# Two-layer gated MLP behind linear attention: the gated product's tiles placed 64 bytes higher in SBUF, with a smaller DMA scratch

## The chip, the cores and the metric

The kernel runs on one core of one Trainium2 chip. The metric is the device time of one execution in microseconds; before the change three runs took 992.68, 993.05 and 998.37 us, with a median of 993.05 us.

## What is computed

Attention with an exponential feature map gives 2304 tokens of 512 values (4 sequences of 576 tokens, 8 heads of 64). Two gated layers follow, each with three weight matrices of 512 x 1536, 512 x 1536 and 1536 x 512. All is in float32.

```python
def _moe_ref(x, w_gate, w_val, w_out):        # layer 1
    g = x @ w_gate
    silu = g * (1.0 / (1.0 + np.exp(-g)))
    val = x @ w_val
    return (silu * val @ w_out).astype(np.float32)

def _moe2_ref(x, w_gate, w_val, w_out):       # layer 2
    gate = 1.0 / (1.0 + np.exp(-(x @ w_gate)))
    val = x @ w_val
    return (gate * val @ w_out).astype(np.float32)

x = attention(q, k, v, w_phi)                 # 2304 x 512
return _moe2_ref(_moe_ref(x))
```

## The kernel before, in words

The attention takes the first 150 us or so and the two gated layers the rest. Each layer is done in two passes over the tokens, one for each half of its 1536 hidden values, so there are four passes, `hh` = 0 to 3; `hh` 0 and 1 are layer 1, `hh` 2 and 3 are layer 2. A pass goes through five blocks of tokens, four of 512 and one of 256, and in each block through three groups `p` of 256 hidden values. A block and a group make a **unit**, so a pass has twelve full units and three half units, and the two layers have the same units in the same number.

A unit has two kinds of matrix multiplication on TensorE. Every float32 factor is held as a high and a low tile of type float32r (names ending in `h` and `l`), and every product is made of three matmuls: high by high, high by low, low by high.

- **Products** (line 1024, `product`): x by `w_gate` and x by `w_val`, in a form with seven block products instead of eight. A full unit has 84 of them, a half unit 48. The stationary operand is a 128 x 128 piece of the tiles `w0h`, `w0l`, `w1h`, ... `w2l`; the moving one is 256 columns of `xh` or `xl`. They write PSUM banks `a` and `b`.
- **Output matmuls** (lines 1099 and 1101, `accumulate`): the gated product of the unit before, held in the tiles `uh0`, `ul0`, `uh1`, `ul1`, by the output weights `o0h` ... `o2l`, into the PSUM banks `c` and `d`. A full unit has 24, in trains of 12, 9 and 3 that stand between groups of 48, 12 and 24 products. In layer 1 (line 1099) the output weights are stationary and 512 columns of `u` move (256 in the small block). In layer 2 (line 1101) 128 columns of `u` are stationary and 512 columns of the output weights move:

```python
if hh < 2:
    nc.tensor.matmul(ps[:, :n], a[:, k], x, start=st, stop=sp)   # line 1099: o stationary, u moves
else:
    nc.tensor.matmul(ps, x[:, k], a, start=st, stop=sp)          # line 1101: u stationary, o moves
```

Between the two, ScalarE copies, gates and rounds (lines 1044, 1062, 579) and VectorE adds, multiplies and takes the low parts (lines 1050, 1067, 573). The tiles that they share with TensorE are `c0` and `c1` (products and their sums) and the four `u` tiles. All six come from the pool `u`, which is opened at line 468, behind the pools of the weights (`w0`, `w1`), of the staging pieces and of the first set of x tiles (`x0`). The pool of the second set of x tiles (`x1`) is opened on top of it when the attention's tiles are gone; `w2` is on the other side of SBUF.

The order of all instructions is written out in a table of times (`TIMES`), and each engine works through its own in that order. Every DMA is issued by SyncE's queue.

A matmul that begins while the next one's stationary piece is being loaded reads SBUF at the same time as that load: the moving columns of one matmul and the stationary columns of the one behind it. "Place" below is a tile's byte address in a partition modulo 256, as the built programs have it. All slices that the matmuls take begin at multiples of 512 bytes into their tile, so that a tile's place is the place of every operand in it.

Of the kernel before, what the change touches and what calls it, by code (L numbers as in the profile page):

```python
# [10 lines left out]
F32 = mybir.dt.float32  # L11
# [9 lines left out]
P = 128  # L21
# [432 lines left out]
def body(ctx: ExitStack, tc: tile.TileContext, qT, kT, v, w_phi2, wpk, out):  # L454
    nc = tc.nc
# [9 lines left out]
    pools = {w: ctx.enter_context(tc.tile_pool(name=w, bufs=1)) for w in ("w0", "w1")}  # L465
    stage = ctx.enter_context(tc.tile_pool(name="stage", bufs=1))
    pools["x0"] = ctx.enter_context(tc.tile_pool(name="x0", bufs=1))
    pools["u"] = ctx.enter_context(tc.tile_pool(name="u", bufs=1))

    xT = [dram.tile([KC, P, S], F32, name=f"xT{b}") for b in range(B)]  # L470
    den = [dram.tile([H, S], F32, name=f"den{b}") for b in range(B)]
# [836 lines left out]
```

## Time and profile before

| | |
|---|---|
| median of three runs | 993.05 us |
| the profiled execution | 996.62 us, of which 994.5 us are its span |
| TensorE (PE) busy | 980.9 us, 99% of the span |
| TensorE weight loads (PEld) | 891.5 us, 90% |
| VectorE (DVE) / ScalarE (ACT) | 692.4 us, 70% / 527.2 us, 53% |
| granted TensorE clock | 1.00 of full speed, the 2.4 GHz level |

Matmuls are pipelined: one begins some 110 to 240 ns after the one before it, and lasts longer than that. So the rate of TensorE is read from the starts in the timeline, and not from the duration of one. The time between two starts is called an interval here. Two starts of the timeline that stand n matmuls apart, divided by n, give the mean interval over them; the timeline has starts to 0.01 us.

### The profile page before, as it was taken

How to read it: one execution, taken by the hardware profiler on the slowest of the kernel's cores; microseconds unless marked ns; L12 is line 12 of the kernel's file. 1: busy time of each engine (PE TensorE's matmuls, PEld its weight loads, DVE VectorE, ACT ScalarE, POOL GpSimd, SP SyncE). 2: the span in 40 equal slices, each digit the busy share in tenths (PEclk: the TensorE clock that was granted, in tenths of full speed). 3: DMA queues.
4: the chain of work that ended last, by engine and by line, in shares of the span. 5: the costliest groups of instructions: out<-in, count | busy, mean ns of one | idle time of the engine just before them, and what ended most of it. 6: DMA issues, size and time to landing. Idle time of an engine off the chain costs nothing.

```text
span 994.5 us, 20911 instructions
## 1 busy us (share of the span) xinstructions
PE 980.9 (99%) x8632; PEld 891.5 (90%) x8632; DVE 692.4 (70%) x1220; ACT 527.2 (53%) x977; POOL 38.8 (4%) x40
## 2 busy tenths in 40 slices
PE   7999999999999999999999999999999999999998
PEld 6777778999999999999999999999999999999997
DVE  6999888938757795368787897486677834555343
ACT  5988977535545564264454574455546534334321
POOL 1433210000000000000000000000000000000000
PEclk9999999999999999999999999999999999999999
DMA  7566876436535532066554442446416002132011
GB/s 239 167 216 211 262 240 197 149 126 182 196 118 153 183 96 83 1 198 213 155 174 134 167 156 77 141 141 197 144 70 191 23 21 86 64 128 86 1 44 42
DMA packets 67551, 136.00 MB, mean 137 GB/s; under 512 B 9408, under 2 KB 35712, under 8 KB 67456
## 3 DMA queue, kind: packets, MB, share of 16 engines
q1 hardware_dynamic: 67456, 134.68, 42.4%
q8 instruction: 67, 1.10, 0.4%
q14 instruction: 28, 0.23, 0.1%
HBM read 94.66 MB, written 39.99 MB: 135 GB/s over the span
## 4 chain that ended last, share of the span: by engine, by line
PE 95%; DVE 3%; DMA 1%; ACT 0%; issue 0%; SPq 0%; DVEq 0%; ACTq 0%
PE a L1024 30%; PE b L1024 23%; PE c L1101 8%; PE c L1099 8%; PE d L1099 8%; PE d L1101 6%; PE d L787 5%; PE c L724 3%; PE w L688 3%; DVE sub L697 1%; DVE m L695 1%; PE w L751 1%; DMA xT<-nd 1%; DMA x<-kT 0%; ACT eq L771 0%
## 5 line engine op out<-in xcount | busy, mean ns | idle before, releaser
L1050 DVE TENSOR_TENSOR c<-b,c 128x512 f32<-128x512 f32 x96 | 66.0, 687 | 118.9 <-PE b L1024 109.9
L1062 ACT ACTIVATE c<-c 128x256 f32<-128x256 f32 x96 | 50.3, 525 | 147.0 <-DVE c L1050 147.0
L1044 ACT COPY c<-a 128x512 f32<-128x512 f32 x96 | 56.4, 587 | 111.9 <-PE a L1024 109.3
L573 DVE TENSOR_TENSOR ul<-c,uh 128x512 fp32r<-128x512 f32 (+1 forms) x120 | 75.8, 635 | 33.3 <-ACT uh L579 32.5
L579 ACT CAST uh<-c 128x512 fp32r<-128x512 f32 (+1 forms) x120 | 69.3, 580 | 41.6 <-DVE c L1067 33.3
L1024 PE MATMUL a<-xh,w0h 128*128 128x256 f32 x288 | 80.7, 280 | 0.0
L1024 PE MATMUL a<-xh,w1h 128*128 128x256 f32 x288 | 80.5, 280 | 0.0
L1024 PE MATMUL a<-xh,w2h 128*128 128x256 f32 x288 | 80.5, 279 | 0.0
L1024 PE MATMUL a<-xl,w0h 128*128 128x256 f32 x288 | 80.3, 279 | 0.0
L1024 PE MATMUL a<-xl,w2h 128*128 128x256 f32 x288 | 80.3, 279 | 0.0
L1024 PE MATMUL a<-xl,w1h 128*128 128x256 f32 x288 | 80.3, 279 | 0.0
L1024 PE MATMUL a<-xh,w0l 128*128 128x256 f32 x288 | 80.2, 279 | 0.0
L1024 PE MATMUL a<-xh,w2l 128*128 128x256 f32 x288 | 80.2, 279 | 0.0
L1024 PE MATMUL a<-xh,w1l 128*128 128x256 f32 x288 | 80.2, 278 | 0.0
L1067 DVE TENSOR_TENSOR c<-c 128x256 f32<-128x256 f32 (+1 forms) x96 | 52.9, 555 | 29.4 <-ACT c L1062 29.4
L1024 PE MATMUL b<-xh,w0h 128*128 128x256 f32 x224 | 62.5, 279 | 0.0
L1024 PE MATMUL b<-xh,w0l 128*128 128x256 f32 x224 | 62.4, 279 | 0.0
L1024 PE MATMUL b<-xh,w2l 128*128 128x256 f32 x224 | 62.4, 279 | 0.0
L1024 PE MATMUL b<-xh,w1l 128*128 128x256 f32 x224 | 62.4, 279 | 0.0
L1024 PE MATMUL b<-xl,w0h 128*128 128x256 f32 x224 | 62.4, 279 | 0.0
L1024 PE MATMUL b<-xh,w1h 128*128 128x256 f32 x224 | 62.4, 278 | 0.0
L1024 PE MATMUL b<-xl,w1h 128*128 128x256 f32 x224 | 62.4, 278 | 0.0
(183 smaller groups left out, 3028.5 us busy)
## 6 DMA issues: line engine op xcount, KB each, us to landing
raw<-wpk SPq DMA_DIRECT2D x72, 512.0 KB, 5.0
wf<-wcv SPq DMA_DIRECT2D x40, 256.0 KB, 2.8
a<-wf SPq DMA_DIRECT2D x20, 512.0 KB, 5.3
b<-xo SPq DMA_DIRECT2D x16, 512.0 KB, 6.1
part<-o SPq DMA_DIRECT2D x13, 512.0 KB, 6.2
o<-part SPq DMA_DIRECT2D x13, 512.0 KB, 4.7
wfo<-wcv SPq DMA_DIRECT2D x20, 256.0 KB, 4.9
v<-v SPq DMA_DIRECT2D x18, 264.0 KB, 7.3
```

What stands on the lines that cost most here:

```text
L573: nc.vector.tensor_tensor(out=lo, in0=src, in1=hi, op=ALU.subtract)
L579: nc.scalar.copy(hi, src)
L688: nc.tensor.matmul(r["ps"][:, i, n, c], r["x"][d, c, n * P:(n + 1) * P], w2[d], start=True, stop=True)
L724: nc.tensor.matmul(kv[qd, b][h // 2][u * 64:(u + 1) * 64, c * P:c * P + VW], e[r0:r1, h % 2, n, h // 2, s, u], r["v"][r0:r1, n, h], start= ...
L787: nc.tensor.matmul(pn[i * w:(i + 1) * w, :m], f, e[:, h, c, :m], start=(c == 0), stop=(c == 1))
L1024: nc.tensor.matmul(o, f[:, c], x[:, c], start=k == first and w == 0 and c == 0 and m == 0, stop=c == 1 and m == 2, skip_group_check=True)
L1044: nc.scalar.copy(part_of(r, d), parts(r, src))
L1050: nc.vector.tensor_tensor(out=c, in0=parts(r, "zy x"[d]), in1=c, op=ALU.add)
L1062: nc.scalar.activation(o, g, AF.Silu if hh < 2 else AF.Sigmoid)
L1067: nc.vector.tensor_tensor(out=o, in0=v, in1=places(r, j, 0, d)[1], op=ALU.mult)
L1099: nc.tensor.matmul(ps[:, :n], a[:, k], x, start=st, stop=sp)
L1101: nc.tensor.matmul(ps, x[:, k], a, start=st, stop=sp)
```

## The change

Three lines open room in SBUF, and one makes the DMA scratch smaller:

```diff
     pools["u"] = ctx.enter_context(tc.tile_pool(name="u", bufs=1))
+    pools["u"].tile([P, 16], F32, name="gap")
+    rest = ctx.enter_context(tc.tile_pool(name="rest", bufs=1))
+    rest.tile([P, 112], F32, name="rest")
...
-    nc = bacc.Bacc("TRN2", target_bir_lowering=False, num_devices=1)
+    nc = bacc.Bacc("TRN2", target_bir_lowering=False, num_devices=1, dynamic_dma_scratch_size=1024)
```

`gap` is 64 bytes in a partition at the start of the pool `u`, and `rest` 448 bytes behind it; no instruction reads or writes them. The scratch shrinks from 16384 to 1024 bytes in a partition, so that everything allocated from the left moves down by 15360 bytes, which is 60 x 256. The places are then:

| tiles | place before | place after |
|---|---|---|
| product weights `w0h` ... `w2l` (stationary, line 1024) | 128 | 128 |
| `xh`, `xl` (moving, line 1024), both sets | 64 | 64 |
| `uh0`, `ul0`, `uh1`, `ul1` (gated product) | 64 | 128 |
| `c0`, `c1` | 64 | 128 |
| output weights `o0h` ... `o2l` | 128 | 128 |

The instructions of every engine and their order are the same in both programs, with the same waits between them; only addresses differ. What that makes of each pair "columns that move, and the stationary piece that is loaded for the matmul behind", as the difference of their places (moving less stationary):

| pair | before | after |
|---|---|---|
| product, then product (both layers) | -64 | -64 |
| layer 1: product, then output | -64 | -64 |
| layer 1: output, then output | -64 | 0 |
| layer 1: output, then product | -64 | 0 |
| layer 2: product, then output | 0 | -64 |
| layer 2: output, then output | +64 | 0 |
| layer 2: output, then product | 0 | 0 |

## Rows read from the trace of the kernel before

**Rows 1.** The page: busy time by engine; the chain that ended last.

```profile
PE 980.9 (99%) x8632; PEld 891.5 (90%) x8632; DVE 692.4 (70%) x1220; ACT 527.2 (53%) x977; POOL 38.8 (4%) x40
...
PE 95%; DVE 3%; DMA 1%; ACT 0%; issue 0%; SPq 0%; DVEq 0%; ACTq 0%
```

**Rows 2.** What TensorE waited for ahead of line 1024: us, times.

```profile
  issue: 1.0, 2
  DVE c L1050: 0.2, 1
```

**Rows 3.** Line 1024 in layers 1 and 2: window, its us, PE busy, PEld busy, clock.

```profile
169.00:589.00 420.00, 282.05 (x2289) 279.48 (x2290) 1.00 0.45 144
589.00:984.00 395.00, 266.31 (x2214) 264.92 (x2212) 1.00 0.28 94
```

**Rows 4.** Timeline of PE, layer 1: start us, duration us, engine, line, out<-in.

```profile
299.25 0.39 PE L1099 MATMUL d<-uh,o0h 128*128 128x512 f32 x1
299.47 0.40 PE L1099 MATMUL d<-ul,o0h 128*128 128x512 f32 x1
...
299.94 0.28 PE L1024 MATMUL a<-xh,w2h 128*128 128x256 f32 x1
...
302.76 0.39 PE L1099 MATMUL c<-uh,o1h 128*128 128x512 f32 x1
...
305.56 0.28 PE L1024 MATMUL a<-xh,w2h 128*128 128x256 f32 x1
...
311.21 0.39 PE L1099 MATMUL c<-uh,o1h 128*128 128x512 f32 x1
...
313.31 0.28 PE L1024 MATMUL a<-xh,w2h 128*128 128x256 f32 x1
...
314.67 0.39 PE L1099 MATMUL d<-uh,o1h 128*128 128x512 f32 x1
```

**Rows 5.** Timeline of PE, layer 2, the same places of a unit.

```profile
706.20 0.39 PE L1101 MATMUL c<-o0h,uh 128*128 128x512 f32 x1
...
708.95 0.28 PE L1024 MATMUL a<-xh,w1h 128*128 128x256 f32 x1
...
709.54 0.28 PE L1024 MATMUL a<-xh,w1l 128*128 128x256 f32 x1
...
714.42 0.39 PE L1101 MATMUL c<-o0h,uh 128*128 128x512 f32 x1
...
716.25 0.39 PE L1101 MATMUL d<-o0l,uh 128*128 128x512 f32 x1
716.48 0.28 PE L1024 MATMUL a<-xh,w1h 128*128 128x256 f32 x1
...
717.86 0.39 PE L1101 MATMUL d<-o0h,uh 128*128 128x512 f32 x1
```

**Rows 6.** Timeline of PE: layer 2's first train, and the six products behind it.

```profile
590.88 0.40 PE L1101 MATMUL c<-o0h,uh 128*128 128x512 f32 x1
...
593.68 0.28 PE L1024 MATMUL a<-xh,w1h 128*128 128x256 f32 x1
...
594.15 0.28 PE L1024 MATMUL a<-xl,w1h 128*128 128x256 f32 x1
```

**Rows 7.** Timeline of PE: the first product of five units, equal numbers of units apart.

```profile
181.88 0.28 PE L1024 MATMUL a<-xh,w2h 128*128 128x256 f32 x1
...
377.44 0.28 PE L1024 MATMUL a<-xh,w1h 128*128 128x256 f32 x1
...
588.05 0.28 PE L1024 MATMUL a<-xh,w1h 128*128 128x256 f32 x1
...
603.27 0.28 PE L1024 MATMUL a<-xh,w2h 128*128 128x256 f32 x1
...
794.02 0.28 PE L1024 MATMUL a<-xh,w1h 128*128 128x256 f32 x1
```

**Rows 8.** DMA queues: packets, MB, share of 16 engines.

```profile
q1 hardware_dynamic: 67456, 134.68, 42.4%
```

## The prediction, made before the changed kernel ran

> **What bounds the kernel now.** I read the page first. TensorE is busy for 99% of the span, and 95% of the chain that ended last is its own work [rows 1]. Next I read what it waited for ahead of the products, line 1024: 1.2 us in the whole run [rows 2]. So nothing that VectorE, ScalarE or a DMA does a little faster or slower moves the end; the time is the sum of TensorE's intervals, and those have to be read from starts.
>
> The two layers have the same units. From the first product of a unit to the first product fifteen units later, layer 1 takes 588.05 - 377.44 = 210.61 us and layer 2 takes 794.02 - 588.05 = 205.97 us; fourteen units take 377.44 - 181.88 = 195.56 and 794.02 - 603.27 = 190.75 us [rows 7]. Layer 1 thus loses 4.64 + 4.81 = 9.45 us against layer 2, at an equal clock of 1.00 [rows 3]. Where does it lose them? The windows over line 1024 say most of it: the time covered by products, divided by their number, is 282.05 / 2289 = 123.2 ns in layer 1 and 266.31 / 2214 = 120.3 ns in layer 2 (tails of trains included, so these are no intervals, but their difference of 2.9 ns can be used) [rows 3].
>
> The timeline shows what kind of loss it is. In a unit of layer 1 the 24 products behind the train of three take 302.76 - 299.94 = 2.82 us, 117.5 ns each; the 48 behind the train of twelve take 311.21 - 305.56 = 5.65 us, 117.7 ns each; the twelve behind the train of nine take 314.67 - 313.31 = 1.36 us, 113.3 ns each [rows 4]. Same line, same shape, same places, no wait. So the products run at one of two rates, and each group keeps the rate into which the train of output matmuls ahead of it put it. In layer 2 the 48 behind the train of twelve take 714.42 - 708.95 = 5.47 us: the first five take 0.59 us, 118 ns each, and the other 43 take 4.88 us, 113.5 ns each; the twelve behind the train of nine take 1.38 us, 115 ns each [rows 5]. There every train leaves the products at the fast rate after some five slow intervals. Even layer 2's first train, which comes out of slow products and runs at 2.80 / 12 = 233 ns a matmul, does so: the next products take 0.47 us for four and are then fast [rows 6].
>
> The trains differ less. A train of twelve takes 305.56 - 302.76 = 2.80 us in layer 1, 233 ns a matmul [rows 4], and 708.95 - 706.20 = 2.75 us in layer 2, 229 ns [rows 5].
>
> **The change, part by part.** No instruction is added, removed or moved, and no wait. Three things could cost or give.
>
> The scratch: all traffic of the kernel's own DMAs is on the hardware queue q1 [rows 8], every one is issued by SyncE, and POOL issues none, so I see no user of the scratch. I take 0 us; the work that would hide a slower transfer is TensorE's unbroken run, with 1.2 us of waits [rows 2].
>
> VectorE and ScalarE on `c` and `u` tiles 64 bytes up: were they to get slower, they have 30% and 47% of the span free [rows 1], and TensorE does not wait for them. 0 us.
>
> The reads of TensorE: here the change acts. A train in layer 1 is left by columns of `u` at 64 that move while product weights at 128 are loaded (-64); after the change both are at 128 (0). That is the pair by which layer 2's trains are left today, which end in the fast rate, whichever way they were entered [rows 5, 6]. And products behind products stay at -64 in both layers, so both rates stay as they are. I therefore price layer 1's products at layer 2's: 2289 x 2.9 ns = 6.6 us off. Lower bound: the state of the train also depends on its own pairs, which are new, so the gain may be nothing. Upper bound: all products at 113.3 ns at once, without the five slow starters; a full unit of layer 2 has 48 + 12 + 24 products, in 5.47 + 1.38 us and, for the 24, 0.59 us for five and 19 x 0.1135 us, together 9.60 us, against 84 x 0.1133 = 9.52 us. That is 0.08 us a unit on top. A layer has 24 full units and six half units of 48 products, 27.4 full units' worth, so both layers at most 54.8 x 0.08 = 4.4 us.
>
> The trains themselves run at a difference of 0 inside, and no row shows that for a whole train. Bounds: the shortest interval of such a matmul is 299.47 - 299.25 = 0.22 us, which I read as 225 ns [rows 4], the longest mean 233 ns [rows 4, 6]; a slower one is not excluded. The nearest row is the last matmul of a train in layer 2, with 0: 716.48 - 716.25 = 0.23 us [rows 5]. I take 231 ns for all. Layer 1 has 24 x 24 = 576 such matmuls (and 144 of 256 columns in the half units, which I leave as they are) and gains 576 x 2 = 1.2 us; layer 2 has 576 and six times twelve, 648, and loses 648 x 2 = 1.3 us. Together 0.1 us lost.
>
> Layer 2's entry into a train changes from 0 to -64, which is what layer 1 has today. An interval of the fast products ahead is 113 ns in both layers, so I take 0 us.
>
> Sum: 996.6 (the profiled execution) - 6.6 + 0.1 = 990.1 us, or 0.9935 of it. The median of the runs is 993.05 us; the same share of it is 986.6 us. I round to **986.5 us**.
>
> A rule speaks against all of this. The Trainium skill, page "TensorE: Matmul & The Clock Gate", section "Step-by-step: what each phase is for", has TensorE read the moving columns and the weights through two independent ports, so that a weight load takes nothing from the running matmul; "SBUF — State Buffer", section "Who interferes with whom", puts it as "PE and ACT never wait on anyone". By that rule the sum is 0 us. The trace does not agree with it in full: 113.3 and 117.7 ns for the same matmul in one unit [rows 4]; but it does not show either that places are the reason.
>
> **The rivals.**
>
> *No effect.* This is what the rule of the two pages would give; as a mechanism of this kernel, the two rates come from something that places do not touch, or layer 1's trains still end in the slow rate. For it: the two rates occur at the very same places [rows 4], so a place alone does not decide; the last difference of 0 in layer 2 stands with stationary and moving tiles exchanged, and that exchange may be what makes the fast exit. Against it: layer 2's trains end fast every time, from two different entries [rows 5, 6]. Time: 993 us, within 3.5 us.
>
> *Slower.* A difference of 0 inside a train is the worst overlap, and trains of both layers end in the slow rate. Place: the exit of each train of layer 2. It decides if the products behind the trains there take 117.7 ns instead of 114.3. Price: 84 x 0.1177 - 9.60 = 0.29 us a full unit, 24 units and six half units (48 products each), 27.4 full units' worth: 7.9 us; layer 1's last fast group of twelve turns slow as well, 12 x 4.4 ns x 24 = 1.3 us. That makes 993 + 9.2 = 1002 us with trains as now. With layer 2's trains at 233 ns, the longest mean seen, it is 648 x 4 = 2.6 us more, 1005 us. For it: two of three trains in layer 1 do end slow, by one and the same pair; equal places are as likely as any to be a meeting of the two reads. Against it: the exit by 0 is seen, and fast.
>
> *Faster than my sum.* Trains at 0 go as the shortest interval does, 225 ns, and leave the products at 113.3 ns at once. Trains: 576 x 8 + 648 x 4 = 7.2 us; products 6.6 + 4.4 = 11.0 us. Together 18.2 us: 975 us. For it: a train out of fast products begins with such an interval [rows 4]. Against: later ones of the same train are longer.
>
> **How the numbers follow.** Forecast (3.5 to 9.9 us gained, 983 to 989.5 us): 0.43, the likeliest. No effect or a mixture (within 3.5 us of 993): 0.20. Faster than the sum (over 9.9 us): 0.25. Slower by over 3.5 us: 0.12, most of it over 1%. One per cent, 9.9 us, is about what a measurement of this kernel can tell from no change. So faster 0.25; slower 0.10; within 1% 0.65. The range reaches to the end of the faster case and leaves its last tenth out, 976, and into the slower one, to 999; the forecast's own range is 983 to 989.5.
>
> **What would show it.** Right: in the changed kernel's timeline the 48 products behind a train of twelve in layer 1 take 5.4 to 5.5 us instead of 5.65, and the fifteen units of layer 1 take about 206 to 207 us instead of 210.61. The trains of twelve then take 2.75 to 2.79 us in both layers; beyond 2.83 us my price of a difference of 0 is wrong. Layer 2's fifteen units stay within 1 us of 205.97; if they grow by 4 us, the slower rival holds. If layer 1's 48 products still take 5.65 us, the exit pair was not the cause. If no start moves at all in relation to its neighbours, places have no part in the rate. A new wait ahead of line 1024 would mean that I was wrong to set the shared tiles' move at nothing.

## The result, and the profile after

The changed kernel takes 1000.12 us (median of 14 executions, 999.37 to 1000.64); the kernel before took 994.80 us on the same chip (14 executions, 988.94 to 999.14). The ratio is 1.0055, with a 95% interval of 1.0038 to 1.0073. So it is slower by 5 us, where 986.5 us had been forecast, and just outside the range of 976 to 999 us. One thing stands out beside the median: the executions of before are spread over 10 us, those of after over 1.3 us.

The page of the changed kernel: busy time by engine, and the chain that ended last.

```profile
PE 984.2 (99%) x8632; PEld 898.6 (90%) x8632; DVE 693.0 (69%) x1220; ACT 527.8 (53%) x977; POOL 38.9 (4%) x40
...
PE 93%; DVE 3%; DMA 2%; ACT 1%; issue 1%; SPq 0%; ACTq 0%; DVEq 0%
```

The other engines do the same work in the same time as before [rows 1]; TensorE is longer by 3.3 us, and the span by 3.5 us (994.5 to 998.0). What it waited for ahead of the products (now line 1027; the output matmuls are lines 1102 and 1104): us, times.

```profile
  issue: 1.0, 2
  DVE c L1053: 0.5, 1
```

No new wait has come up; the one on VectorE has grown from 0.2 to 0.5 us [rows 2]. The windows over line 1027, with the columns of [rows 3]:

```profile
169.00:589.00 420.00, 283.75 (x2304) 281.05 (x2304) 1.00 0.46 145
589.00:984.00 395.00, 269.76 (x2183) 268.39 (x2184) 1.00 0.28 93
```

At the same granted clock, 1.00, layer 1's products are where they were (283.75 / 2304 = 123.2 ns, as before), and layer 2's have gone from 120.3 to 269.76 / 2183 = 123.6 ns. The 2.9 ns that were to leave layer 1 have stayed there, and layer 2 has gained 3.3. The timeline of TensorE shows the same in a unit; a train of twelve and the 48 products behind it, in layer 1 and in layer 2:

```profile
302.46 0.39 PE L1102 MATMUL c<-uh,o1h 128*128 128x512 f32 x1
...
305.18 0.28 PE L1027 MATMUL a<-xh,w2h 128*128 128x256 f32 x1
...
310.83 0.39 PE L1102 MATMUL c<-uh,o1h 128*128 128x512 f32 x1
...
705.40 0.39 PE L1104 MATMUL c<-o0h,uh 128*128 128x512 f32 x1
...
708.12 0.28 PE L1027 MATMUL a<-xh,w1h 128*128 128x256 f32 x1
...
713.78 0.39 PE L1104 MATMUL c<-o0h,uh 128*128 128x512 f32 x1
```

The train takes 2.72 us in both layers, 226.7 ns a matmul, where it took 2.80 and 2.75 us [rows 4, 5]. The 48 products take 5.65 and 5.66 us, 117.8 ns each: as in layer 1 before, and 0.19 us more than layer 2's 5.47 us. From 182 us on, all products behind trains of 512 columns go at this rate in both layers, with one exception that shows the rule. Early in layer 2 one interval in the first group of 48, at 593.90 us, is 0.13 us long:

```profile
594.14 0.28 PE L1027 MATMUL a<-xh,w1l 128*128 128x256 f32 x1
...
596.64 0.39 PE L1104 MATMUL c<-o0h,uh 128*128 128x512 f32 x1
...
597.34 0.39 PE L1104 MATMUL c<-o0h,uh 128*128 128x512 f32 x1
...
598.70 0.28 PE L1027 MATMUL a<-xh,w1h 128*128 128x256 f32 x1
...
600.11 0.39 PE L1104 MATMUL d<-o0h,uh 128*128 128x512 f32 x1
```

Behind it the products go at the fast rate (22 intervals from 594.14 to 596.64 us, 113.6 ns each). The train that follows takes 0.70 us for its first three matmuls and 1.36 us for the other six, 226.7 ns each, and the twelve products behind it take 1.41 us: 117.5 ns, slow again. So a train of 512 columns at difference 0 settles at 226.7 ns, whether the products ahead went at 117.8 or at 113.6 ns, and hands on the slow rate.

The half units of layer 1 behave otherwise. Their trains have the same three differences as those of its full units (entry -64, inside 0, exit 0), but 256 columns move, and the products behind them end in the fast rate, 113.7 to 115.0 ns on the mean of a group. Here are 48 of them:

```profile
276.13 0.29 PE L1027 MATMUL a<-xh,w0h 128*128 128x256 f32 x1
...
281.59 0.28 PE L1102 MATMUL c<-uh,o2h 128*128 128x256 f32 x1
```

They take 5.46 us, where 48 in a full unit take 5.65. One and the same exit by 0 thus leaves products at 117.8 ns behind the one kind of train and near 114 ns behind the other.

Where the time goes, in us, from the same unit starts as in [rows 7] (the last three of after are 376.70, 585.53 and 794.58; two experiments from below stand beside it):

```profile
376.70 0.28 PE L1027 MATMUL a<-xh,w1h 128*128 128x256 f32 x1
...
585.53 0.28 PE L1027 MATMUL a<-xh,w1h 128*128 128x256 f32 x1
...
794.58 0.28 PE L1027 MATMUL a<-xh,w1h 128*128 128x256 f32 x1
```

| stretch | before | after | l1_only | l1_as_l2 |
|---|---|---|---|---|
| to layer 1's first unit counted here | 181.88 | 182.75 | 183.52 | 183.00 |
| layer 1, fourteen units | 195.56 | 193.95 | 193.91 | 192.16 |
| layer 1, fifteen units | 210.61 | 208.83 | 208.83 | 206.23 |
| layer 2, fifteen units | 205.97 | 209.05 | 206.16 | 206.00 |
| the rest of layer 2, to the end | 200.48 | 203.42 | 200.48 | 200.41 |
| span | 994.5 | 998.0 | 992.9 | 987.8 |

After against before: layer 1 gains 1.61 + 1.78 = 3.39 us, layer 2 loses 3.08 + 2.94 = 6.02 us, and 0.87 us are lost ahead of both, 0.46 of them ahead of the very first product (149.82 against 150.28 us), in the attention, whose instructions the change leaves as they were. In the profiled executions of all the kernels with this attention the first product starts between 149.07 and 151.81 us, so this part is not put down to the change. The sum is 3.50 us, the whole difference of the spans.

By kind, with the intervals between starts added up: in layer 1, 2220 products went from 260.45 to 260.13 us and 550 output matmuls of 512 columns from 127.93 to 124.78 us; in layer 2, 2220 products went from 253.79 to 261.38 us and 645 output matmuls from 147.77 to 146.25 us. The trains give 4.7 us; layer 2's products take 7.6.

### The profile page after: what moved, and what is told of

It reads as the page before. It is cut to its first block, busy times and chain, and to the rows that moved or that the text cites. A ratio compares the mean times of both kernels' runs of the same rounds, so it can differ in the third digit from the quotient of the medians.

```text
span 998.0 us, 20911 instructions
## 1 busy us (share of the span) xinstructions
PE 984.2 (99%) x8632; PEld 898.6 (90%) x8632; DVE 693.0 (69%) x1220; ACT 527.8 (53%) x977; POOL 38.9 (4%) x40
## 4 chain that ended last, share of the span: by engine, by line
PE 93%; DVE 3%; DMA 2%; ACT 1%; issue 1%; SPq 0%; ACTq 0%; DVEq 0%
PE a L1027 30%; PE b L1027 24%; PE c L1104 8%; PE c L1102 7%; PE d L1102 7%; PE d L1104 6%; PE d L790 4%; PE w L691 3%; PE c L727 3%; DVE sub L700 1%; DVE m L698 1%; DMA raw<-wpk 1%; DMA den<-nd 1%; PE w L754 1%; DMA x<-kT 0%
## 5 line engine op out<-in xcount | busy, mean ns | idle before, releaser
L1027 PE MATMUL b<-xh,w2h 128*128 128x256 f32 x224 | 62.9, 281 | 0.0
L1027 PE MATMUL b<-xl,w2h 128*128 128x256 f32 x224 | 62.9, 281 | 0.0
```

What stands on the lines that cost most here:

```text
L1027: nc.tensor.matmul(o, f[:, c], x[:, c], start=k == first and w == 0 and c == 0 and m == 0, stop=c == 1 and m == 2, skip_group_check=True)
```

## The experiments

**The intervals by themselves.** A kernel that leaves the whole computation out: one tile of weights, one of columns, chains of 30 matmuls on TensorE and nothing else, with 256 or 512 columns at a place that differs from the weights' by so many bytes. Ahead of a chain stand 1, 3, 5 or 7 matmuls of another length, so that it begins at another moment.

```diff
+    def chain(n, s, count=REP):
+        for k in range(count):
+            nc.tensor.matmul(b[:, :n], w[:, (k % 4) * P:(k % 4 + 1) * P],
+                             m[:, s + 512 * (k % 3):s + 512 * (k % 3) + n], start=True, stop=True)
```

> A kernel that leaves the whole computation out: on TensorE alone it runs chains of 30 float32r matmuls, 256 or 512 columns moving, with the moving columns 0, 64, 128, 192, 32, 96 or 256 bytes (modulo 256) past the place of the stationary pieces, each chain behind 1, 3, 5 or 7 odd-sized matmuls that shift its start; then groups of 24 with trains of 12, 9 and 3 for all 16 pairs of four differences. Nothing else reads SBUF meanwhile. Theory (the place difference and the moment of the start together set the interval): 512 columns at 0 take 226.7 ns each whatever the start; at -64 (192) 231 and 236 in turn; at +64 226, 229, 232 in turn or 233. 256 columns at -64 take 113.3 or 117.8 ns by their start; at 0 about 120 ns, as the small block's output matmuls of the changed kernel do; 256 bytes behaves as 0. Rival (the two rates come from what the other engines and the DMAs read and write, not from TensorE's own two reads): one interval for each size at all differences, near 113 and 216 to 226 ns.

Six of its chains in the windows view (window, its us, PE busy, granted clock, DMA share, GB/s); each window goes from the start of a chain's twelfth matmul to that of its last, 18 intervals: 256 columns at 0, at 192 twice; 512 columns at 0, 64 and 192.

```profile
29.33:31.49 2.16, 2.16 (x20) 1.00 0.00 0
77.17:79.29 2.12, 2.12 (x20) 1.00 0.00 0
81.22:83.26 2.04, 2.04 (x21) 1.00 0.00 0
147.29:151.37 4.08, 4.08 (x19) 1.00 0.02 4
177.59:181.71 4.12, 4.12 (x20) 1.00 0.02 4
239.09:243.29 4.20, 4.20 (x19) 1.00 0.00 0
```

Divided by 18 these are 120.0, 117.8, 113.3, 226.7, 228.9 and 233.3 ns. All differences, with the four starts of each:

| difference | 256 columns, ns | 512 columns, ns |
|---|---|---|
| 0 and 256 | 119.8 or 120.0 | 226.7 |
| 32 | 116.4 to 116.7 | 233.2 to 233.4 |
| 64 | 117.8 | 228.9 |
| 96 | 120.0 | 233.3 |
| 128 | 118.9 or 120.0 | 232.0 to 232.7 |
| 192 (-64) | 113.3 from one start, 117.8 from three | 233.3 |

So place differences do set the interval, with nothing else running: the "no effect" rival falls. Two rates at one and the same difference are there too, and what stands ahead of the chain, and with it the moment at which it starts, chooses between them. And no difference is good for everything: 0 is the best one for 512 columns and, with 96, the worst of the table for 256.

Behind these chains the kernel has groups of 24 products between trains of 12, 9 and 3. With products at 192 and trains at 0, as in layer 1 of the changed kernel, all products take 117.8 ns and the trains, but for the first, 226.7. With trains at 192 as well, as in layer 1 before, products are fast behind the trains of 12 and 3 and slow behind those of 9.

**The scratch alone.**

```diff
-    nc = bacc.Bacc("TRN2", target_bir_lowering=False, num_devices=1)
+    nc = bacc.Bacc("TRN2", target_bir_lowering=False, num_devices=1, dynamic_dma_scratch_size=1024)
```

> The smaller DMA scratch alone; all places modulo 256 as before. Theory (only the places of the u tiles matter): ratio to the kernel before 1.000 within 0.3%, products and trains at the same intervals as before (117.7 or 113.3 ns; trains 233 and 229 ns). Rival (the scratch or the absolute addresses matter): 1.005 as for the whole change, trains at 226.7 ns or some DMA later.

996.45 us (991.87 to 997.51) against 996.64 us, ratio 1.0006 (0.998 to 1.0032): no difference. But its profiled execution shows where a spread like that of before can come from, since it fell into another state of the same places. Its timeline: 48 products behind a train of twelve; a wait; 48 behind the next train of twelve; twelve behind the train of nine.

```profile
203.39 0.28 PE L1024 MATMUL a<-xh,w0h 128*128 128x256 f32 x1
...
208.83 0.39 PE L1099 MATMUL c<-uh,o2h 128*128 128x512 f32 x1
...
362.11 0.50 PE L1099 MATMUL c<-ul,o2h 128*128 128x512 f32 x1 [0.19 <-DVE ul L573]
...
364.78 0.28 PE L1024 MATMUL a<-xh,w0h 128*128 128x256 f32 x1
...
370.43 0.39 PE L1099 MATMUL c<-uh,o2h 128*128 128x512 f32 x1
...
372.53 0.28 PE L1024 MATMUL a<-xh,w0h 128*128 128x256 f32 x1
...
373.89 0.39 PE L1099 MATMUL d<-uh,o2h 128*128 128x512 f32 x1
```

Ahead of the wait the 48 take 5.44 us (113.3 ns), and the 24 behind the train of three are fast and the twelve slow; behind the wait the 48 take 5.65 us and the twelve 1.36 us (113.3 ns), as in [rows 4]. The intervals of the trains tell why. In layer 1 a train alternates between 231 and 236 ns; one that ends on 236 leaves the products fast, one that ends on 231 leaves them slow. Entered from slow products it begins 231, 229, 236, entered from fast products 226, 236. So out of slow products an odd train ends fast and an even one slow; out of fast products an even one ends fast and an odd one slow. With trains of 12, 9 and 3 this gives 12 of 84 products fast (the twelve behind the nine), or, when a wait has turned it over, 72 of 84 (all but the twelve). The rule holds for all 69 trains of 512 columns that stand between products of layer 1 in the profile of before, and for 67 of 69 here. The two that break it are the train with the wait shown and one of twelve at 185.4 us, which turns the rate from slow to fast without a wait. In the profile of before, on the other hand, a train at 364.5 us has its second matmul 0.26 us late, and nothing turns. So a wait can turn the state over, but need not, and it is not the only thing that does.

**Lengths of the trains.** If parity decides, trains of even length in layer 1 keep the fast rate once they have it. The places are those of before; a delay in the table of times turns 12, 9, 3 into 12, 6, 6.

```diff
+            if fn.__name__ == "accumulate" and args[1] < 2 and args[-1] == "0":
+                t += 170
+            if fn.__name__ in ("out_sum", "out_store") and args[0] < 2:
+                t += 120
```

> The kernel before, places and scratch as they were; in layer 1 three output matmuls of each unit are issued behind the last product group instead of ahead of it, so that the trains are 12, 6 and 6 long instead of 12, 9 and 3 (and the sums and stores of layer 1 1.2 us later in the plan). Theory: at -64 a train of even length leaves the rate as it found it, and one of odd length turns it over; so in layer 1 products keep one rate for a whole pass, all 113.4 ns or all 117.7, where now 12 of 84 (or 72 of 84) are fast. The rate of a pass is set by its first train and by single waits, so executions fall on levels: a pass all fast saves about 84 x 4.4 ns x 13.7 units = 5 us against all slow. 986 to 997 us, with products at 113.4 ns behind several trains on end, or none at all. Rival (the length of a train has no part; it is which banks or weights the train ends on): the share of fast products stays 12 of 84, behind the second train of each unit, and the time 994 to 997 us.

989.64 us (988.45 to 995.72) against 993.89 us, ratio 0.9952 (0.9929 to 0.9975). In the profiled execution the first pass is fast from 181.9 us on in all groups but two, 36 products behind a wait at 280 us, and the second is slow from 363.7 us on; 48 products in each, from the timeline:

```profile
318.35 0.28 PE L1028 MATMUL a<-xh,w0h 128*128 128x256 f32 x1
...
323.80 0.39 PE L1103 MATMUL c<-uh,o2h 128*128 128x512 f32 x1
...
363.71 0.28 PE L1028 MATMUL a<-xh,w0h 128*128 128x256 f32 x1
...
369.36 0.39 PE L1103 MATMUL c<-uh,o2h 128*128 128x512 f32 x1
```

5.45 and 5.65 us: the rate is kept through 66 of 69 trains, in either state, as parity has it. Three trains turn it over: one of six at 177.2 us, with a wait behind it, and two of twelve without idle time, at 285.3 us (slow to fast) and at 360.9 us (fast to slow). What turned those two the trace does not show.

**Everything at one place.** The x tiles moved to 128 as well, so that products too stand at 0.

```diff
     pools["x0"] = ctx.enter_context(tc.tile_pool(name="x0", bufs=1))
+    pools["x0"].tile([P, 16], F32, name="xgap")
```

> The x tiles are moved 64 bytes up as well, so that u, x, the product weights and the output weights all lie at 128; scratch as before. Every pair is then at a difference of 0. Theory: trains at 226.7 ns as in the changed kernel; products at 0 go as the small block's output matmuls of 256 columns did there, about 120 ns each, so (120 - 117.5) x 4600 = 11 us above the changed kernel, about 1011 us. Rival (equal places are good for every matmul, as for the trains): products at 113.3 ns, (117.5 - 113.3) x 4600 = 19 us below it, about 981 us.

1014.36 us (4 executions), ratio 1.0186 (1.0157 to 1.0214). Products take 119.7 ns on the mean, as the chains have it for 0. Trains take 229.7 ns and not the 226.7 expected: their first five intervals are longer (some 233, 236, 229, 232 and 231 ns), and only then come 226.7. The rival that equal places are good for all pairs falls.

**The gated product at 192.** This tells the exit pair from the pairs ahead of it: layer 1's exit becomes +64, layer 2's exit stays 0 as before. The scratch is the small one.

```diff
+    pools["u"].tile([P, 32], F32, name="gap")
+    rest = ctx.enter_context(tc.tile_pool(name="rest", bufs=1))
+    rest.tile([P, 96], F32, name="rest")
```

> The u and c tiles are moved 128 bytes instead of 64 (u at 192, output weights at 128): in layer 1 outputs stand at +64 to outputs and products, in layer 2 at -64 inside a train and at 0 to the product behind it. Theory: the layers exchange what they had inside the trains: layer 1's trains take 229 ns (+64), layer 2's 231 and 236 in turn (-64); layer 2's trains still leave the products by 0. If the exit by 0 decides the products' rate, layer 2 keeps 114.5 ns; if the pairs inside the train decide, layer 2's products behind trains of 12 and 3 go to 117.7 ns as layer 1's did, and layer 1's get fast. The total is then near the kernel before, 993 to 997 us, either way. Rival (it is being equal that matters, and nothing else): as the kernel before in every interval.

1003.08 us (4 executions), ratio 1.007 (1.0042 to 1.0098), a miss. Layer 1's products are slow throughout. Layer 2's are mixed; the 48 products behind the train of twelve, in two units that follow each other:

```profile
610.65 0.28 PE L1027 MATMUL a<-xh,w2h 128*128 128x256 f32 x1
...
616.30 0.39 PE L1104 MATMUL c<-o1h,uh 128*128 128x512 f32 x1
...
626.14 0.28 PE L1027 MATMUL a<-xh,w0h 128*128 128x256 f32 x1
...
631.61 0.39 PE L1104 MATMUL c<-o2h,uh 128*128 128x512 f32 x1
```

5.65 us in the one, 5.47 us in the other, and 115.9 ns on the mean of all, although the pair by which these trains are left is the one of before. So the exit pair alone does not decide; what comes ahead of it in the train does too. The pair by which the train is entered changed as well here (0 to -128): with the exit kept, no choice of the two tiles' places changes the pairs inside a train without it, so these two are not told apart.

**Units of trains and products.** Again without the computation: twelve, 48, nine, twelve, three and 24 matmuls as in a unit, for 16 combinations of places. Ahead of them stand chains as above at 144 to 240 bytes: eight bytes to either side of 192, at 184 and 200, 256 columns take 120.0 to 122.1 ns, and none of the eight differences gives less than 116.7; 512 columns take 230.0 to 236.7 ns. "Stationary" and "moving" are the places of a train's operands less that of the product weights; products stand at -64 throughout.

```diff
+                        chain(512, b, 12, a)
+                        chain(256, 48, 48)
+                        chain(512, b, 9, a)
+                        chain(256, 48, 12)
+                        chain(512, b, 3, a)
+                        chain(256, 48, 24)
```

> As the run pairs, the whole computation left out. First the same chains at finer differences: 144, 160, 176, 184, 200, 208, 224 and 240 bytes. Then the order of a full unit (trains of 12, 9 and 3 of 512 columns between 48, 12 and 24 products), with products at -64 as in the real kernel, for all 16 combinations of the places of the stationary and the moving tile of the trains, from two starts. Theory (difference and moment of the start set each interval): only near -64 is there a fast product of 113.3 ns; trains whose columns lie 0 past their own stationary tile take 226.7 ns; the combination of layer 2 before the change (stationary at the x tiles' place, moving at the weights') leaves fast products behind every train, as in the real kernel, and that of layer 1 before the change only behind trains of odd length out of slow products or of even length out of fast ones; that of the changed kernel (both at the weights' place) leaves 117.8 ns for good. Rival (the real kernel's layers differ for another reason than places): layer 2's combination leaves the same share of slow products here as layer 1's.

Four units in the windows view: the combination of the changed kernel (0, 0), that of layer 1 before (0, 192), the best one (128, 192) and that of layer 2 before (192, 0).

```profile
430.70:446.04 15.34, 15.34 (x111) 1.00 0.00 1
632.96:648.13 15.17, 15.17 (x111) 1.00 0.00 1
1173.21:1188.27 15.06, 15.06 (x111) 1.00 0.00 1
1239.99:1255.09 15.10, 15.10 (x111) 1.00 0.00 1
```

| stationary, moving | us a unit | trains | products |
|---|---|---|---|
| 128, 192 | 15.05 at every start | 229 | fast behind every train |
| 192, 0 (layer 2 before) | 15.09; 15.34 the first time | 229 | fast behind every train |
| 0, 192 (layer 1 before) | 15.17 | 232 to 233 | 72 of 84 fast |
| 0, 0 (changed kernel) | 15.33 to 15.35 | 226.7 | all slow |
| 0, 64 (layer 1 of the kernel at 192) | 15.42 | 230 to 235 | all slow |
| 64, 0 (layer 2 of the kernel at 192) | 15.16 or 15.48 | 231 to 234 | by start |

The four combinations in which a train's two places are equal take 15.29 to 15.43 us, and all four leave the 48 and the twelve products slow from both starts. In two of them, (0, 0) and (64, 64), the trains are the fastest of all, at 226 to 228 ns, and the products behind cost more than that saves. A full unit of layer 2 loses 15.33 - 15.09 = 0.24 us by the change; 24 of them make 5.8 us, and layer 2 lost 6.02.

**The change in layer 1 alone.** The `u` tiles get 256 spare bytes, and layer 1 takes them 64 bytes up; layer 2 has them where they were. This kernel and the two that follow have the small scratch.

```diff
+            k = 16 if hh < 2 else 0
+            r["u", f] = [pools["u"].tile([P, 2 * NQ + 64], R32, tag=f"u{x}{f}",
+                                         name=f"u{x}{f}")[:, k:k + n] for x in "hl"]
```

> The change in layer 1 alone: the gated product lies 64 bytes up in layer 1 (trains there at difference 0) and as before in layer 2. The theory: layer 1 as in the changed kernel (trains 226.7 ns, 3.5 us less; products 117.8 ns, 1.4 us more; the small block's 256-column output matmuls 120), layer 2 as before (products 113.8 to 114.3, trains 229): 994 - 2 = 992 us, so that the whole loss of the changed kernel, and more, is layer 2's. The rival (layer 2's rate is what layer 1 hands on, or the loss is layer 1's): 998 to 1001 us.

994.29 us (993.21 to 995.53, 12 executions) against 996.24 us, ratio 0.9987 (0.9968 to 1.0007). The timing alone is a tie, and with the changed kernel at 1.0055 (its interval lies wholly above this one) it says that the loss is layer 2's. The unit starts say it to a tenth of a microsecond:

```profile
377.43 0.28 PE L1024 MATMUL a<-xh,w1h 128*128 128x256 f32 x1
...
586.26 0.28 PE L1024 MATMUL a<-xh,w1h 128*128 128x256 f32 x1
...
792.42 0.28 PE L1024 MATMUL a<-xh,w1h 128*128 128x256 f32 x1
```

Fifteen units take 208.83 us in layer 1, as in the changed kernel, and 206.16 us in layer 2, as in the kernel before up to 0.2. So what layer 1 hands on is not what slowed layer 2 down.

**Layer 1 at layer 2's places.** Output weights at 64 and gated product at 128 in layer 1, so that both operands of a train have the places that they have in layer 2; layer 2 is left alone.

```diff
+    def out_weight(pool, hh, p, x):
+        v = pool.tile([P, 2 * DM + 64], R32, tag=f"o{p}{x}", name=f"o{p}{x}{hh}")
+        k = 48 if hh < 2 else 0
+        return v[:, k:k + 2 * DM].rearrange("p (f n) -> p f n", f=2)
...
+            k = 16 if hh < 2 else 0
+            r["u", f] = [pools["u"].tile([P, 2 * NQ + 64], R32, tag=f"u{x}{f}",
+                                         name=f"u{x}{f}")[:, k:k + n] for x in "hl"]
```

> Layer 1 alone is moved: there the output weights lie at 64 and the gated product at 128, so that a train's stationary tiles stand at 64 and its moving ones at 128, the two places that they have in layer 2, where nothing is changed. The theory: layer 1's trains fall from 232.8 to 229 ns (2.2 us) and its products keep the fast rate behind every train as in layer 2, 117.2 to 113.8 (7.8 us): 994 - 10 = 984 us; pairs2 gives 15093 ns a unit, 40 more than both64, so within about 1 us of it. The rival (what stands in the tiles decides, not where they lie: layer 1's stationary tiles are weights, layer 2's are gated products): layer 1 stays, 992 to 997.

989.27 us (988.71 to 989.81, 8 executions) against 996.24 us, ratio 0.9947 (0.9924 to 0.9969). It beats both kernels, and its executions lie within 1.1 us of each other. The unit starts:

```profile
375.16 0.28 PE L1022 MATMUL a<-xh,w1h 128*128 128x256 f32 x1
...
581.39 0.28 PE L1022 MATMUL a<-xh,w1h 128*128 128x256 f32 x1
...
787.39 0.28 PE L1022 MATMUL a<-xh,w1h 128*128 128x256 f32 x1
```

Fifteen units take 206.23 us in layer 1 and 206.00 us in layer 2: the two layers are alike at last. Layer 1 gains 7.8 us against the profiled execution of before; its start was 1.1 us later, in the attention, and so the span is 6.7 us shorter. The expected 984 us were too low by 5. The trains of 512 columns gave 1.8 us of the 2.2 expected, and those of 256 another 0.3; the products came down to 114.7 ns and not to 113.8, which makes 5.8 us instead of 7.8, and the kernel before had 996.24 us as its median in these runs and not 994.

**The best combination in both layers.** As above with 32 and 48 in place of 48 and 0 for the output weights, and 0 and 48 in place of 16 and 0 for the gated product: in both layers a train's stationary tiles lie at 0 and its moving ones at 64.

> The gated product's and the output weights' tiles get 256 spare bytes each, and a layer takes them at an offset: in both layers the stationary tiles of the output matmuls now lie at place 0 and the moving ones at 64 (w at 128 and x at 64 as before). Of the 16 combinations in pairs2 this one took the least per unit of 12, 48, 9, 12, 3 and 24 (15053 ns, at every start). The theory (place differences and the start moment set the rates): products near 113.5 ns in both layers and trains near 229 ns, so layer 1's 2304 products lose 117.2 - 113.5 = 3.7 ns each (8.5 us), its 576 output matmuls 232.8 - 229 = 3.8 ns (2.2 us), layer 2 keeps its times: 994 - 10.7 = 983 us, and executions that agree within 3 us since no train leaves the fast rate. The rival (in the real kernel waits and the other engines set the rate, whatever the places): 992 to 997.

987.68 us (985.14 to 991.42, 6 executions) against 996.24 us, ratio 0.9925 (0.9898 to 0.9951): the lowest median of all, with an interval that overlaps that of the kernel above, and more than the 983 us expected. 48 products in two units of layer 1:

```profile
235.05 0.28 PE L1022 MATMUL a<-xh,w2h 128*128 128x256 f32 x1
...
240.71 0.40 PE L1104 MATMUL c<-uh,o1h 128*128 128x512 f32 x1
...
290.39 0.28 PE L1022 MATMUL a<-xh,w1h 128*128 128x256 f32 x1
...
295.84 0.39 PE L1104 MATMUL c<-uh,o0h 128*128 128x512 f32 x1
```

5.66 us in the one, 5.45 us in the other. There is a second steady state here that none of the starts in the chains had met: trains at 233.5 ns that leave the products slow. The first pass falls into it at 185.8 us without a wait, the second at a wait of 0.26 us at 363 us, and the small block in the middle (256-column output matmuls) turns each to the pattern that leaves the products fast. That is a miss of the claim that this combination is the same from every start, and of the 3 us within which the executions were to agree: they span 6.3. In the small block twelve of those output matmuls, at +64, take 1.36 us, 113.3 ns each, where all four chains at 64 took 117.8: four starts do not show every state of a difference.

## Why the prediction was wrong, point by point

- **The bound.** Right: TensorE's intervals set the time, no new wait came up, and the scratch and the engines that share the tiles cost nothing that can be measured.
- **The step that failed: the exit by 0 leaves layer 1's products at layer 2's fast rate (6.6 us off).** It gave 0.3 us. Only the half units of layer 1 went as forecast and gained 1.3 us; in the full units all products are slow, and the twelve behind the trains of nine, fast before, lost 1.0. The prediction took the pair at the end of the train as what decides the rate, from the fact that layer 2's trains are left by that pair and end fast. Its own rows spoke against that: by one exit pair, -64, layer 1's trains of twelve and three left slow products and its trains of nine left fast products [rows 4]. What the runs show in its place is that the whole train counts, and the state in which it is entered: trains of 512 columns at difference 0, 226.7 ns a matmul, leave slow products in both layers of the changed kernel, whichever rate they come from. That the kernel with the gated product at 192 keeps layer 2's exit and loses its fast rate shows it from the other side. The prediction had named this doubt ("the state of the train also depends on its own pairs, which are new") and had used it in the sum only as the bound of no gain.
- **Layer 2's products untouched.** The same step, with a loss: 253.79 to 261.38 us, 7.6 us. The place and the price of the rival "Slower" (exits of layer 2, 117.7 in place of 114.3 ns, 7.9 us) are what happened. It had been given a chance of 0.12. Layer 2's fifteen units grew by 3.1 us and not by 4, since their trains became shorter by 0.8 us meanwhile.
- **The trains at 0: mis-sized.** 231 ns were taken, 226.7 were measured, within the bounds of 225 and 233 ns. The term was 0.1 us lost and came out as 4.7 us gained. The reason that the rival "Slower" gave, 0 as the worst overlap inside a train, was wrong with it: 0 is the best difference for 512 columns in the chains.
- **Layer 2's entry at 0 us.** No run tells that pair from the pairs inside the train.
- **The sum as it was measured:** -0.3 and +7.6 for the products, -4.7 for the trains, +0.1 for the small block, and 0.9 ahead of the units counted: 3.6 us, against 3.5 of span. The medians differ by 5.3 us, because the profiled execution of before, at 996.6 us, lay 1.8 above the median. Layer 1 ran with 12 of 84 products fast in it; that the faster executions ran in the other state is inferred from the profile of the kernel with the small scratch, since they have no profiles of their own.
- **"Fifteen units of layer 1 in 206 to 207 us"** is what layer 1 takes when it is given both of layer 2's places and not only layer 2's exit (206.23 us). The gain that was forecast was there; this change does not fetch it.

The chain kernel settles the rule that spoke against any effect. With nothing but TensorE at work, the same matmul of 256 columns takes 113.3 to 120.0 ns by the difference of two addresses and by its start. The Trainium skill, page "TensorE: Matmul & The Clock Gate", section "Step-by-step: what each phase is for", says that moving columns and weights come through two independent ports; the measurement differs from the conclusion that a load takes nothing from the running matmul, and it decides.

## What to carry to other kernels

Where TensorE never waits, read the intervals between its starts, group by group: two rates of one instruction at one place mean that the state at the start of the group matters, and then a pair of operands that looks fast in one context is no evidence for another. Before tiles are moved, run the kernel's own order of matmuls for all combinations of places in a kernel without the computation, and then in the whole kernel, because states turn up there that the small one does not meet. A spread of 1% between executions of one program may come from such a state. The kernel with layer 1 at layer 2's places, which in its profile is back at the fast rate soon after each wait, takes 0.5% less than the kernel before, and its executions lie within 1.1 us.

## What the runs showed of the hardware that was not expected

- The interval of a matmul depends on the place, modulo 256 bytes, of the moving columns against that of the next stationary piece, and on the start: 113.3 to 122.1 ns for 256 columns, 226.7 to 236.7 ns for 512, at a granted clock of 1.00 and without another engine at work. A difference of 256 bytes is the same as 0. (For 256 columns the chains shifted the moving tile alone; for 512 the units of trains shifted both.)
- Six of the steady patterns add up to multiples of 6.67 ns: 113.3 is 17 of them, 120.0 is 18, 226.7 is 34, three intervals of 117.8 are 53, three of 228.9 are 103, two of 233.3 are 70. A pattern that closes after two or three matmuls ends at another point for each length of a train, which would give the rule of odd and even trains. That is an inference from these sums and not shown; no run shifted a start by a known few ns.
- The same program can run layer 1 in two states, 12 or 72 of 84 products fast, and change between them, at a wait of 0.2 us or without one. The difference is about 3.6 us a pass (195.56 us for fourteen units in the profile of before, 191.99 us in that of the kernel with the small scratch).
- Open: what turned trains over without a wait (at 285.3 and 360.9 us in the kernel with even trains, at 185.4 us in that with the small scratch), and why the combination (128, 192) has a second state in layer 1 of the whole kernel and none in the chains.
